# Attention over hop tokens in half-array products, and one iteration's statements in a written order

## The chip, the cores and the metric

One core of a Trainium2 chip runs the whole program. The metric is the device time of one execution in microseconds (us). The kernel before took 3996.6 us, the median of three runs from 3993.74 to 4000.15 us. The profile shows one execution, of 3999.62 us, with a span of 3997.8 us.

## The reference, cut to what matters

A graph of 10,000 nodes and 160,000 edges. Seven normalized propagations make seven more token rows for each node beside its input row, so each node has eight tokens of 128 numbers. One attention block runs over the eight tokens of each node by itself, and a second softmax weighs the eight results into one row.

```python
tok = jnp.stack(toks, axis=1)                      # (N, 8, 128)
t = _layernorm(tok)
q, key, v = t @ wq, t @ wk, t @ wv
attn = softmax(q @ key.T * scale)                  # 8 x 8 in each node
o = tok + (attn @ v) @ wo
r = _layernorm(o)
alpha = softmax(r @ w_r)                           # over the 8 tokens
return einsum('nk,nkd->nd', alpha, o)
```

## The kernel before, in words

The program has two stages. The class `Hops` makes the seven propagations, with the token rows written to `tok` in device memory; the change does not touch it. Behind it the function `attention` runs, and the change is all there, but for a few constants that are made during the hops.

`attention` works on groups of 16 nodes, which with eight tokens each fill 128 partitions (partition = 8 x node + token). Sixteen groups make a supergroup (`SG = 16`); there are 625 groups, so the list `sgs` has 40 supergroups, the first with one group and the others with sixteen. The loop at L1168 is a software pipeline over them. In iteration `i` it

- starts the loads of the token rows of supergroup `i+3` on the SyncE queue (`load`),
- transposes supergroup `i+1` on TensorE (`xT`, four parts of four groups) and ScalarE copies each part out of PSUM,
- for `i` makes the values (`val`, six parts of up to three groups, `xT` as the stationary operand and `Wv` as the moving one; columns 128 to 130 of `Wv` give three extra numbers for each token), the rows `uT` (four parts), the sums of squares (`squares`, sixteen ScalarE activations with an accumulator), and the scores (`score`, 32-column tiles of the array, four nodes to a tile),
- for `i-1` makes the softmax on VectorE (`soft1a`, `soft1b`, `soft2`, `soft2b`) with the exponential on ScalarE (`soft_exp`), spreads the weights by GpSimd over a product with `in4` (tile `p`, 32 wide), transposes the 32x32 blocks on VectorE, and has GpSimd copy the four diagonal blocks of each group into a 128x128 tile `PT` that is zero elsewhere (`soft3`, L1071),
- for `i-2` multiplies `PT` with the values (`attend`, sixteen 128x128x128 products) and adds the tokens on VectorE (`resid`, L989),
- for `i-3` takes the statistics of the result (`stats`, sixteen VectorE instructions), and the inverse roots for `i` and `i-3` together (`norms`, `root`, `norms2`),
- for `i-4` makes the second softmax (`read1`, `read_exp`, `read2`), and for `i-5` the weighted sum (`read3`, 32-column tiles) and the store.

The order of the work is that of the Python statements (`tc.manual_schedule`): each engine takes its instructions in the order in which they are written, and waits on semaphores where one needs another engine's result. `same_node` is a product that gives each row a sum over the eight rows of its node, in 32-column tiles (tile `sm`). PSUM has eight banks: three for `pt`, `pv` and `pu` together, two for `po`, and one each for `ps`, `sm` and `pf`.

Of the kernel before, what the change touches and what calls it, by code (L numbers as in the profile page):

```python
# [36 lines left out]
BIG = 32768.0  # L37

# [793 lines left out]
class Attention:  # L832
# [3 lines left out]
    def __init__(self, ctx, tc, tab, tok, ws, ngrp=N // 16):  # L836
        self.tc, self.nc, self.tok, self.ws = tc, tc.nc, tok, ws
        r = ngrp % SG
        self.sgs = [(0, r)] * (r > 0) + [(s, SG) for s in range(r, ngrp, SG)]

        y = [t.bitcast(F32)[:, a:a + SG, :] for t in tab[::-1] for a in range(0, NT - SG + 2, SG)]
        self.xb, self.ob = y[:6], y[6:]
        cp = ctx.enter_context(tc.tile_pool(name="acp", bufs=1))
        for name, w in (("M", 128), ("Wv", 131), ("id8", 8), ("in4", 4), ("sel", 16), ("same", 128), ("ident", 128)):
            setattr(self, name, cp.tile([128, w], F32, name=name))

# [3 lines left out]
    def load(self, i, ks=range(8), queue=None):  # L850
        s, n = self.sgs[i]
        for k in ks:
            src = bass.AP(tensor=self.tok[k].tensor, offset=self.tok[k].offset + s * 16 * 128, ap=[[n * 128, 16], [128, n], [1, 128]])
            (queue or self.nc.sync).dma_start(self.x(i)[k::8, :n, :], src)

    def constants(self, ctx, pw, ident):
# [3 lines left out]
        M, Wv, id8, in4, sel, same = self.M, self.Wv, self.id8, self.in4, self.sel, self.same  # L860
# [11 lines left out]
        pn, pk, pq = (cp.tile([128, 1], I32, name=n) for n in ("pn", "pk", "pq"))  # L872
# [3 lines left out]
        nf, kf, qf = (cp.tile([128, 1], F32, name=n) for n in ("nf", "kf", "qf"))  # L876
        for f, i in ((nf, pn), (kf, pk), (qf, pq)):
            V.tensor_copy(f, i)
# [5 lines left out]
        V.tensor_scalar(in4, cf[:, :4], qf, None, op0=ALU.is_equal)  # L884
        V.tensor_scalar(sel, cf, nf, None, op0=ALU.is_equal)
# [23 lines left out]
def attention(ctx, att, out):  # L909
# [7 lines left out]
    M, Wv, id8, in4, sel, same, ident = att.M, att.Wv, att.id8, att.in4, att.sel, att.same, att.ident  # L917
# [8 lines left out]
    PT, AB = [], []  # L926
    for i in range(2):
        p = cp.tile([128, SG, 128], F32, name=f"pT{i}")
        G.memset(p, 0.0)
        PT.append(p)  # L930
        a = cp.tile([128, SG, 32], F32, name=f"Ab{i}")
        G.memset(a, 0.0)
        AB.append(a)
# [30 lines left out]
    def val(i, c):  # L964
        a, b = 3 * c, min(3 * c + 3, sgs[i][1])
        if c == 0:
            S[i]["v"] = vp.tile([128, SG, 131], F32, name="v")
        if a >= b:
            return
        p = pp.tile([128, 512], F32, name="pv", tag="a", bufs=3)[:, :393].rearrange("p (g d) -> p g d", d=131)  # L970
        for g in range(a, b):
            T.matmul(p[:, g - a, :], S[i]["xT"][:, g, :], Wv, start=True, stop=True)  # L972
        A.copy(S[i]["v"][:, a:b, :], p[:, :b - a])

    def attend(i, q):
        a, b = 4 * q, min(4 * q + 4, sgs[i][1])
        if q == 0:
            S[i]["o"] = att.ob[i % len(att.ob)]
        if a >= b:
            return  # L980
        p = pp.tile([128, 4, 128], F32, name="po", tag="o", bufs=2)
        for g in range(a, b):
            T.matmul(p[:, g - a, :], PT[i % 2][:, g, :], S[i]["v"][:, g, :128], start=True, stop=True)  # L983
        S[i]["po", q] = p

    def resid(i, q):
        a, b = 4 * q, min(4 * q + 4, sgs[i][1])
        if a < b:
            V.tensor_tensor(S[i]["o"][:, a:b, :], S[i]["po", q][:, :b - a], S[i]["x"][:, a:b, :], op=ALU.add)  # L989

    def squares(i, a, b):

        if a == 0:
            S[i]["sq"] = sp.tile([128, SG], F32, name="sq")
        for g in range(a, min(b, sgs[i][1])):
            j = jp.tile([128, 128], F32, name="junk")
            A.activation(j, S[i]["x"][:, g, :], AF.Square, bias=S[i]["x"][:, g, 0:1], scale=-1.0, accum_out=S[i]["sq"][:, g:g + 1])  # L997

    def score(i):
        p = S[i]["s"] = pp.tile([128, SG, 32], F32, name="ps", tag="s", bufs=1)  # L1000
        for g in range(sgs[i][1]):
            for c in range(0, 128, 32):
                T.matmul(p[c:c + 32, g, :], S[i]["uT", g // 8][:, g % 8, c:c + 32], S[i]["xT"][:, g, c:c + 32],
                         start=True, stop=True, tile_position=(0, c))
# [6 lines left out]
    def extras(i):  # L1011

        n = sgs[i][1]
        r = wp.tile([128, 2, SG, 8], F32, name="rb")
        V.tensor_tensor(r[:, 0, :n], S[i]["rs"][:, :, None].to_broadcast([128, n, 8]), id8[:, None, :].to_broadcast([128, n, 8]), op=ALU.mult)
        V.tensor_tensor(r[:, 1, :n], S[i]["v"][:, :n, 128:129].to_broadcast([128, n, 8]), id8[:, None, :].to_broadcast([128, n, 8]), op=ALU.mult)
        S[i]["rb"] = r


    def soft1a(i):  # L1020
        n = sgs[i][1]
        c = wp.tile([128, SG, 4, 8], F32, name="c4")[:, :n]
        V.tensor_tensor(c, S[i]["s"][:, :n].rearrange("p g (n k) -> p g n k", k=8),
                        in4[:, None, :, None].to_broadcast([128, n, 4, 8]), op=ALU.mult)
        d = wp.tile([128, SG, 2, 8], F32, name="c2")[:, :n]
        V.tensor_tensor(d, c[:, :, 0:2], c[:, :, 2:4], op=ALU.add)
        e = S[i]["e"] = wp.tile([128, SG, 8], F32, name="e")[:, :n]
        V.tensor_tensor(e, d[:, :, 0], d[:, :, 1], op=ALU.add)

    def soft1b(i):  # L1030
        n = sgs[i][1]
        e = S[i]["e"]
        rk = wp.tile([128, SG, 8], F32, name="rk")[:, :n]
        V.tensor_tensor(rk, S[i]["sm"][:, 0, :n], S[i]["rs"][:, :, None].to_broadcast([128, n, 8]), op=ALU.mult)
        V.tensor_mul(e, e, rk)
        m = wp.tile([128, SG], F32, name="m")[:, :n]
        V.tensor_reduce(m, e, axis=X, op=ALU.max)
        V.tensor_tensor(e, e, m[:, :, None].to_broadcast([128, n, 8]), op=ALU.subtract)

    def soft_exp(i):  # L1040
        n = sgs[i][1]
        y = S[i]["y"] = wp.tile([128, SG, 9], F32, name="y")[:, :n]
        A.copy(y[:, :, 8:9], S[i]["v"][:, :n, 129:130])
        A.activation(S[i]["e"], S[i]["e"], AF.Exp)

    def soft2(i):
# [3 lines left out]
        V.tensor_reduce(z, e, axis=X, op=ALU.add)  # L1050
        V.reciprocal(z, z)
        V.tensor_tensor(e, e, S[i]["sm"][:, 0, :n], op=ALU.mult)
        V.tensor_tensor(e, e, z[:, :, None].to_broadcast([128, n, 8]), op=ALU.mult)  # L1053
        p = wp.tile([128, SG, 4, 8], F32, name="p4")[:, :n]
        G.tensor_tensor(p, e[:, :, None, :].to_broadcast([128, n, 4, 8]), in4[:, None, :, None].to_broadcast([128, n, 4, 8]), op=ALU.mult)  # L1055
        S[i]["p"] = p

    def soft2b(i):
# [3 lines left out]
        V.tensor_tensor(y[:, :, :8], S[i]["e"], S[i]["sm"][:, 1, :n], op=ALU.mult)  # L1062
        w = S[i]["w"] = sp.tile([128, SG], F32, name="w")[:, :n]
        V.tensor_reduce(w, y, axis=X, op=ALU.add)

    def soft3(i):
        n = sgs[i][1]
        t = wp.tile([128, SG * 32], F32, name="t4")
        V.transpose(t[:, :n * 32], S[i]["p"].rearrange("p g n k -> p (g n k)"))
        for c in range(0, 128, 32):  # L1070
            G.tensor_copy(PT[i % 2][c:c + 32, :n, c:c + 32], t[c:c + 32, :n * 32].rearrange("p (g k) -> p g k", k=32))  # L1071
# [8 lines left out]
    def norms(i, j):  # L1080
        v = sp.tile([128, 2, SG], F32, name="rv")
        if not (ok(i) and ok(j)) or min(sgs[i][1], sgs[j][1]) < SG:
            V.memset(v, 1.0)
        if ok(i):
            n = sgs[i][1]
            d = sp.tile([128, SG], F32, name="rx")[:, :n]
            V.tensor_mul(d, S[i]["v"][:, :n, 130], S[i]["v"][:, :n, 130])
            V.scalar_tensor_tensor(v[:, 0, :n], S[i]["sq"][:, :n], 1.0 / D, d, op0=ALU.mult, op1=ALU.subtract)
        if ok(j):
            n = sgs[j][1]  # L1090
            st = S[j]["st"][:, :n]
# [206 lines left out]
```

## Time and profile before

| | us |
|---|---|
| median of three runs | 3996.6 |
| the profiled execution, its span | 3999.62, 3997.8 |
| last matmul of the hops starts, first transposition of the attention | 3314.02, 3321.62 |
| score of the third supergroup, score of the last one | 3354.07, 3949.18 |
| busy over the span: PE, DVE, ACT, POOL | 3745.5, 3322.9, 2724.5, 1766.6 |

The attention takes some 680 us at the end of the span. PE is TensorE's matmul row, PEld its weight loads, DVE is VectorE, ACT ScalarE and POOL GpSimd. A row of the timeline gives a start, a busy time, the engine, the line, the operation with its tiles and shapes, and how many instructions are merged in it; the busy time of merged rows reaches beyond the start of the next row, because a matmul's end (and, to a smaller degree, a VectorE instruction's) overlaps with the next one's start. What a row costs its engine is therefore read from its start to the start of the next row.

### The profile page before, as it was taken

The numbers are of one execution on the slowest core, as the hardware profiler recorded it, in microseconds if no ns is written. First come the engines' busy times: TensorE is split into PE (matmuls) and PEld (weight loads), VectorE is DVE, ScalarE is ACT, GpSimd is POOL, SyncE is SP. The second block draws the span as 40 slices with busy tenths as digits, with TensorE's granted clock in tenths as the row PEclk, the third lists the DMA queues.
The fourth block names the chain that finished last, engine by engine and source line by source line (L and its number), as shares of the span: only waits on it lengthen the run. The fifth ranks groups of instructions, "written<-read, shape, count | busy, mean of one in ns | idle before, by whom it ended". The sixth has DMA issues, their size and how long they took to land.

```text
span 3997.8 us, 165094 instructions
## 1 busy us (share of the span) xinstructions
PE 3745.5 (94%) x69690; PEld 3031.4 (76%) x69690; DVE 3322.9 (83%) x6961; ACT 2724.5 (68%) x6830; POOL 1766.6 (44%) x2342
## 2 busy tenths in 40 slices
PE   6886799999989999999999999999999999999997
PEld 4665566666658888888888788878878887788885
DVE  8998999999977777777777777777766666999998
ACT  6884456666666666666666666666665658888884
POOL 0000333333335665666666566656656662222222
PEclk8998899999999999999999999999999999999998
DMA  3100445454556666666666666666656552222220
GB/s 104 32 2 1 134 151 154 149 162 143 156 168 189 201 201 193 202 203 200 193 202 202 185 202 202 202 189 198 202 184 205 186 183 77 74 74 76 78 78 13
DMA packets 321189, 594.93 MB, mean 149 GB/s; under 512 B 56183, under 2 KB 214101, under 8 KB 315189
## 3 DMA queue, kind: packets, MB, share of 16 engines
q1 hardware_dynamic: 282485, 506.62, 40.0%
q0 software_dynamic: 35392, 72.55, 6.3%
q8 instruction: 546, 8.95, 0.9%
q10 hardware_dynamic: 2560, 5.12, 0.4%
q14 instruction: 206, 1.69, 0.1%
HBM read 455.43 MB, written 128.67 MB: 146 GB/s over the span
## 4 chain that ended last, share of the span: by engine, by line
PE 71%; DVE 19%; ACT 4%; issue 2%; DMA 2%; POOL 0%; another core or an unknown queue 0%; SPq 0%; DVEq 0%; ACTq 0%; POOLq 0%
PE p L580 26%; PE acc L556 24%; PE acc L542 4%; DVE w L514 3%; PE pv L972 3%; PE po L983 3%; PE pu L961 3%; DVE ux L219 2%; DVE o L212 2%; ACT rs L340 2%; PE tb L440 2%; PE pt L951 1%; DVE oh L206 1%; DVE R L212 1%; DVE w L511 1%
## 5 line engine op out<-in xcount | busy, mean ns | idle before, releaser
L585 ACT CAST eb<-p 128x512 f16<-128x512 f32 x3065 | 1623.7, 596 | 645.4 <-PE p L580 404.3
L587 DVE TENSOR_TENSOR eb<-p,one 128x512 f16<-128x512 f32 x1912 | 1230.6, 685 | 332.2 <-PE acc L556 195.9
L580 PE MATMUL p<-tab,w 128*32 128x256 f16 x39816 | 1288.7, 274 | 44.2 <-issue 21.4
L556 PE MATMUL acc<-eb,w 128*128 128x256 f16 (+1 forms) x9954 | 1246.9, 274 | 8.4 <-DVE indeg L649 3.1
L580 PEld LDWEIGHTS <-w 128*32 128x32 fp8e4 x39816 | 1002.3, 96 | 261.3 <-issue 225.8
L556 PEld LDWEIGHTS <-w 128*128 128x128 fp8e4 x9954 | 954.3, 98 | 170.3 <-issue 54.9
L526 POOL DMA_INDIRECT og<-tabh,oidx x553 | 613.3, 1109 | 767.7 <-DVE vi L478 389.6
L526 POOL DMA_INDIRECT og<-tabd,oidx x541 | 586.3, 1084 | 640.2 <-PE acc L556 294.3
L625 POOL TENSOR_SCALAR r<-s,ctok 128x128 f32<-128x128 f32 x474 | 294.3, 621 | 47.7 <-DVE s L571 30.3
L616 ACT ACTIVATE tab<-s,c 128x128 f16<-128x128 f32 x395 | 158.6, 402 | 209.7 <-DVE eb L587 185.6
L617 DVE SCALAR_TENSOR_TENSOR tab<-s,c,tab 128x128 f16<-128x128 f32 x395 | 138.9, 352 | 180.8 <-issue 168.0
L571 DVE TENSOR_REDUCE s<-acc 128x128 f32<-128x256 f32 x553 | 228.7, 414 | 24.0 <-PE acc L569 11.2
L997 ACT ACTIVATE junk<-tab 128x128 f32<-128x128 f32 x625 | 245.1, 394 | 0.0
L340 ACT ACTIVATE rs<-iof,rb 128x128 fp8e4<-128x128 f32 x784 | 231.8, 389 | 0.3
L514 DVE TENSOR_TENSOR w<-dsl,iof 128x2432 fp8e4<-128x2432 f16 x79 | 211.5, 2678 | 0.0
L983 PEld LDWEIGHTS po<-v,pT 128*128 128x128 f32 x1250 | 159.5, 194 | 42.1 <-issue 27.7
L525 POOL COPY og<-eb 128x1 f16<-128x1 f16 x452 | 83.9, 186 | 241.7 <-ACT eb L585 241.7
L1055 POOL TENSOR_TENSOR p<-e,in 128x512 f32<-128x512 f32 (+1 forms) x40 | 40.8, 1020 | 321.0 <-DVE e L1053 321.0
L972 PE MATMUL pv<-Wv,xT 128*128 128x131 f32 x1250 | 176.7, 285 | 1.3 <-ACT xT L952 0.6
L983 PE MATMUL po<-v,pT 128*128 128x128 f32 x1250 | 167.0, 277 | 5.5 <-DVE tab L989 4.1
L972 PEld LDWEIGHTS pv<-Wv,xT 128*128 128x128 f32 x1250 | 154.2, 192 | 17.9 <-issue 8.8
L542 PE MATMUL acc<-og,w 128*128 128x256 f16 x553 | 156.8, 284 | 0.0
(285 smaller groups left out, 4611.9 us busy)
## 6 DMA issues: line engine op xcount, KB each, us to landing
w<-gsd SPq DMA_DIRECT2D x474, 592.0 KB
gsd<-w SPq DMA_DIRECT2D x79, 592.0 KB
rb<-srow SPq DMA_DIRECT2D x79, 576.0 KB
tok<-r SPq DMA_DIRECT2D x546, 64.0 KB
tab<-tok SPq DMA_DIRECT2D x273, 128.0 KB
tabd<-tab SPq DMA_DIRECT2D x396, 64.0 KB
og<-tabh,oidx POOLq DMA_INDIRECT x553
og<-tabd,oidx POOLq DMA_INDIRECT x541
```

Source lines behind the costliest of these rows:

```text
L340: A.activation(ro[:, j - a, i, :], self.iof, AF.Abs_reciprocal_sqrt, scale=2.0 ** 21, bias=rb[:, j - VP, i:i + 1], saturate=False)
L514: V.tensor_tensor(w[:, :NJ * 128].rearrange("p (j d) -> p j d", d=128), dsl[:, g, :, None].to_broadcast([128, NJ, 128]), self.iof1[:, None ...
L526: self.nc.gpsimd.indirect_dma_start(out=o, out_offset=None, in_=src[0] if i == NI else src[1], in_offset=bass.IndirectOffsetOnAxis(ap=self ...
L542: T.matmul(acc[0][:, :256], W, og[i], start=start, stop=stop)
L556: T.matmul(acc[0][:, :m], w[:, J * 128:(J + 1) * 128], e[:, j, :m], start=first and J == 0, stop=J == NG - 1 and not (first or late))
L580: T.matmul(p[32 * q:32 * q + 32, j], w[:, NJ * 128 + s * CAP:NJ * 128 + (s + 1) * CAP], tab[:, s, :], start=True, stop=True)
L585: A.copy(e[:, :n, 0:256], pv)
L587: V.tensor_tensor(e[:, :n, 0:256], pv, self.one[:, :, None].to_broadcast([128, n, 256]), op=ALU.mult)
L625: self.nc.gpsimd.tensor_scalar(r, s, ct[:, t:t + 1], None, op0=ALU.mult)
L972: T.matmul(p[:, g - a, :], S[i]["xT"][:, g, :], Wv, start=True, stop=True)
L983: T.matmul(p[:, g - a, :], PT[i % 2][:, g, :], S[i]["v"][:, g, :128], start=True, stop=True)
L997: A.activation(j, S[i]["x"][:, g, :], AF.Square, bias=S[i]["x"][:, g, 0:1], scale=-1.0, accum_out=S[i]["sq"][:, g:g + 1])
```

## The change

Four things.

1. **Products of eight nodes.** A full supergroup's sixteen groups are split into two halves of eight groups. A unit `u = c * 8 + q` holds, on partitions 0 to 63, nodes `8c` to `8c+7` of group `q`, and on partitions 64 to 127 the same nodes of group `8 + q`. `val` writes values in this layout with two 64-column products for each unit, `score` reads its tiles in it, the weights are spread eight wide with `in8` (tile `p8`, 64 numbers for each unit, in place of 32), and VectorE transposes them. The transposed tile `t8` is used directly: a 64x64 block of it is zero off the node's own 8x8 blocks. `attend` makes four 64x64 products, each with 128 moving columns, for each `q`. `PT`, its zeroing and the GpSimd copies are gone.
2. **Regrouping.** Sums of squares are taken by group and the softmax sums by unit, so both go to a tile `R`, and four 64-column products with parts of the identity (`regroup`) bring the one into unit order and the other into group order, in a part of the bank of `pf`.
3. **A written order.** The functions return short steps, and `ORDER` names the order in which one iteration issues them; the loop reads it word by word. `score` and the first step of the softmax now belong to the start of the next iteration, `xT` to its middle.
4. **Smaller things.** The copy of one column of `v` into `y` goes from ScalarE to GpSimd. The first supergroup has two groups, of which one is stored.

```diff
+ORDER = """
+v0 b b s b a0 b q q v1 v2 q v3 b q v4 v5 b b m h b b a1 q b q a2 a3 r0 a4 a5
+a6 e r1 t0 r2 b c0 o00 k q c2 c1 x0 o01 x1 q q c3 f w0 q d0 b d1 b b b q u0 u1 b t1
+o10 w1 n0 q n3 n1 n2 g w2 n4 n5 p n6 x2 x3 u2 u3 o11 q q q y0 y1 z0 z1 z2 z5 z3 q z6 z4
+"""
...
-        self.sgs = [(0, r)] * (r > 0) + [(s, SG) for s in range(r, ngrp, SG)]
+        self.sgs = [(0, 2)] * (r > 0) + [(s, SG) for s in range(r, ngrp, SG)]
...
-    PT, AB = [], []
+    R = []
+    for i in range(6):
+        a = cp.tile([128, 2, SG], F32, name=f"R{i}")
...
     def val(i, b):
-        for g in range(a, b):
-            T.matmul(p[:, g - a, :], S[i]["xT"][:, g, :], Wv, start=True, stop=True)
+        for u in us:
+            c, q = u // m, u % m
+            for h in range(2):
+                T.matmul(p[64 * h:64 * h + 64, u - us[0], :], S[i]["xT"][:, h * m + q, 64 * c:64 * c + 64], Wv,
+                         start=True, stop=True, tile_position=(0, 64 * h))
...
-        p = pp.tile([128, 4, 128], F32, name="po", tag="o", bufs=2)
-        for g in range(a, b):
-            T.matmul(p[:, g - a, :], PT[i % 2][:, g, :], S[i]["v"][:, g, :128], start=True, stop=True)
+        for h in range(2):
+            S[i]["po", s, h] = pp.tile([128, 4, 128], F32, name="po", tag="o", bufs=2)
+        for q in qs:
+            for c in range(2):
+                for h in range(2):
+                    a, z, u = 64 * h, 64 * c, c * m + q
+                    T.matmul(S[i]["po", s, h][z:z + 64, q - 4 * s, :], t[a:a + 64, u * 64:u * 64 + 64], v[a:a + 64, u, :128],
+                             start=True, stop=True, tile_position=(a, z))
...
+    def regroup(out, rr, moves):
+        for m, js in moves:
+            js = slice(js[0], js[-1] + 1)
+            for b in range(2):
+                for a in range(2):
+                    T.matmul(out[64 * a:64 * a + 64, js, b * m:b * m + m], ident[:, 64 * b:64 * b + 64], rr[:, js, a * m:a * m + m],
+                             start=True, stop=True, tile_position=(0, 64 * a))
...
     def soft_exp(i):
-        A.copy(y[:, :, 8:9], S[i]["v"][:, :n, 129:130])
+        G.tensor_copy(y[:, :, 8:9], S[i]["v"][:, :n, 129:130])
...
-        G.tensor_tensor(p, e[:, :, None, :].to_broadcast([128, n, 4, 8]), in4[:, None, :, None].to_broadcast([128, n, 4, 8]), op=ALU.mult)
+            G.tensor_tensor(p, e[:, :, None, :].to_broadcast([128, n, 8, 8]), in8[:, None, :, None].to_broadcast([128, n, 8, 8]), op=ALU.mult)
...
     def soft3(i):
-        t = wp.tile([128, SG * 32], F32, name="t4")
-        V.transpose(t[:, :n * 32], S[i]["p"].rearrange("p g n k -> p (g n k)"))
-        for c in range(0, 128, 32):
-            G.tensor_copy(PT[i % 2][c:c + 32, :n, c:c + 32], t[c:c + 32, :n * 32].rearrange("p (g k) -> p g k", k=32))
+        t = S[i]["t"] = wp.tile([128, SG * 64], F32, name="t8")
+        V.transpose(t[:, :n * 64], S[i]["p"].rearrange("p g n k -> p (g n k)"))
...
+        single = dict(s=(soft, score, i - 1), e=(soft, soft_exp, i - 1), p=(soft, soft3, i - 1), f=(read, read_exp, i - 4),
+                      g=(ok(i - 5), store, i - 5))
+        several = dict(v=(ok(i), val, i), u=(ok(i), uT, i), t=(ok(i - 2), attend, i - 2))
+        lists = dict(a=(soft, soft1, i - 1), c=(soft, soft2, i - 1), d=(soft, soft2b, i - 1), r=(read, read1, i - 4),
+                     w=(read, read2, i - 4), n=(True, norms, i, i - 3), y=(True, root, i), z=(True, rstd, i, i - 3))
+        plain = dict(q=square, b=stat, m=sums, h=weigh, k=move)
```

The words of `ORDER`: `v`, `u`, `x`, `t` are the parts of `val`, `uT`, `xT` and `attend`; `s`, `m`, `h`, `k` are `score`, the node sums, the weighted sum of `read3` and the regrouping; `b` is one of the sixteen statistics and `q` one of the sixteen squares (six of this supergroup ahead of `k`, ten of the next behind it); `o` is `resid`; `a`, `c`, `d` are steps of the first softmax, with `e` its exponential and `p` the transposition; `r`, `f`, `w` are those of the second; `n`, `y`, `z` make the inverse roots; `g` is the store.

More of the change, by code (lines that the diff above doesn't have):

```diff
@@ L1167, in attention @@
     load(1)
+    S += [dict() for _ in range(5)]
+    taken = [0, 0]
     for i in range(-1, n + 5):
@@ L1171, in attention, with square, stat @@
             load(i + 3)
-        if ok(i - 1):
-            soft1a(i - 1)
-        for q in range(4):
+        soft, read = ok(i - 1), ok(i - 4)
+        taken = [taken[1] if i >= 0 else 0, 0]
+        done, current, kept = [0], [0], {}
+        def square():
+            j = current[0]
+            if ok(i + j):
+                squares(i + j, taken[j], taken[j] + 1)
+            taken[j] += 1
+        def stat():
+            if ok(i - 3):
+                stats(i - 3, done[0], done[0] + 1)
+            done[0] += 1
```

337 lines of the change are left out of this document (168 added, 169 removed).

## The prediction

> **What bounds the kernel now.** I read the page's first two parts, then the busy times of a long stretch of the attention, the waits in it, the chain that ended last, and one iteration in order of time. The page says that PE is the busiest engine and that the last fifth of the span, the attention, is another regime than the hops:
>
> ```profile
> PE 3745.5 (94%) x69690; PEld 3031.4 (76%) x69690; DVE 3322.9 (83%) x6961; ACT 2724.5 (68%) x6830; POOL 1766.6 (44%) x2342
> ...
> PE   6886799999989999999999999999999999999997
> DVE  8998999999977777777777777777766666999998
> ACT  6884456666666666666666666666665658888884
> ```
>
> In its steady part (windows, then waits of the same stretch, then the chain's lines behind 3400) the engines stand like this:
>
> ```profile
> 3400.00:3900.00 500.00, 493.06 (x8180) 402.78 (x8179) 474.91 (x1670) 442.34 (x1641) 130.74 (x215) 1.00 0.26 76
> ...
> PE pt L951 <- PE ps L1003: 6.5, 31, 0.3
> ...
> DVE tab L989 <- PE po L983: 0.7, 2, 0.5
> ...
> by line: PE pv L972 18.6%; PE po L983 17.0%; PE pu L961 16.0%; PE pt L951 9.1%; PE ps L1003 5.8%; PE pf L1151 5.6%; DVE st L1078 4.3%; PE sm L1009 4.0%; DVE tab L989 3.2%; issue 1.9%; DMA tab<-in_x 1.3%; DVE rv L1097 0.8%; DVE t L1069 0.7%;
> ```
>
> PE is busy 493 of 500 us, and its one wait is 0.2 us an iteration. The chain is three quarters PE. But VectorE is busy 475 of 500 and waits 0.7 us on PE in all of it: its missing 25 us are seams between its own instructions. So both are full, and ScalarE (442) is close. A gain on PE counts only if VectorE shrinks with it. The period comes from the scores of the third and the last supergroup, 37 iterations apart: (3949.18 - 3354.07) / 37 = 16.08 us.
>
> ```profile
> 3354.07 1.62 PE L1003 MATMUL ps<-xT,uT 128*32 128x32 f32 x128
> ...
> 3949.18 1.30 PE L1003 MATMUL ps<-xT,uT 128*32 128x32 f32 x128
> ```
>
> **PE, term by term.** Most of one iteration's matmuls, to be read from start to start:
>
> ```profile
> 3606.70 1.05 PE L983 MATMUL po<-v,pT 128*128 128x128 f32 x8
> 3607.59 0.60 PE L951 MATMUL pt<-ident,tab 128*128 128x128 f32 x4
> 3608.03 1.88 PE L961 MATMUL pu<-xT,M 128*128 128x512 f32 x4
> 3609.75 1.05 PE L983 MATMUL po<-v,pT 128*128 128x128 f32 x8
> 3610.73 1.30 PE L1003 MATMUL ps<-xT,uT 128*32 128x32 f32 x128
> 3612.24 0.63 PE L951 MATMUL pt<-ident,tab 128*128 128x128 f32 x4 [0.22 <-PE ps L1003]
> 3612.71 0.83 PE L972 MATMUL pv<-Wv,xT 128*128 128x131 f32 x6
> 3613.47 0.64 PE L1009 MATMUL sm<-rb,same 128*32 128x256 f32 x8
> 3613.93 0.40 PE L1009 MATMUL sm<-lb,same 128*32 128x128 f32 x8
> 3614.26 0.94 PE L972 MATMUL pv<-Wv,xT 128*128 128x131 f32 x6
> 3615.13 1.08 PE L1151 MATMUL pf<-tab,Ab 128*32 128x128 f32 x32
> 3616.14 0.94 PE L972 MATMUL pv<-Wv,xT 128*128 128x131 f32 x6
> 3616.91 1.05 PE L983 MATMUL po<-v,pT 128*128 128x128 f32 x8
> ```
>
> *Attend.* Eight matmuls take 3607.59 - 3606.70 = 0.89 us, 0.111 each; an iteration has 32 (sixteen products, two passes each), 3.56 us. After, there are 64 quarter-size ones (eight `q`, four tiles, two passes) with the same 128 columns. Four tiles of 32 columns do run side by side here: the 32 of `pf` take 1.01 us, 0.13 for each round of four. If the four 64x64 tiles do so too, attend is 16 rounds of 0.111, 1.78 us: a gain of 1.78. No row here shows tiles that share columns and differ in rows, so the bounds are 1.78 gained and nothing gained (only the column halves overlap); a serial array would lose 3.56. I take the first, nearest to the `pf` row.
>
> The Trainium skill (TensorEngine Tiling (Array Packing), Key Properties) says that different tiles can load weights and multiply in parallel, and counts four independent ones at 64x64, which would give the 1.78. No run here shows it yet.
>
> *Val.* Twice as many matmuls, of 64 columns, two at a time over 131 moving columns: 32 rounds as before, no change. Score, sums, `read3`, `xT` and `uT` keep their counts.
>
> *Changes of tile shape.* They cost here: the eight `po` ahead of the scores take 0.98 instead of 0.89, the six `pv` ahead of the sums 0.76, and behind `read3` 0.77, instead of 0.67 (6 x 0.111); the 32 of `pf` take 0.14 more than eight rounds of 0.109. That is 0.09 to 0.10 into, and 0.14 plus 0.10 out of, a small shape: about 0.33 a pair, 0.165 each. Before, six in an iteration; after (v0, s, v1, m, t0, k, x0, t1, x2) nine: +0.5. Against it, the first transposition's wait behind the scores (0.22, for the loads' semaphores) now comes behind `k` and can go. Net +0.3, bounds 0 and +0.6.
>
> *Regroup.* Two products on each column half, two passes each, make four rounds of 16 columns. The scores' 32 rounds of 32 columns take 1.51, 0.05 each, so 0.2, to 0.4 if each costs a `pf` round; I take 0.25. It also makes PE wait for the last two squares before it, with x0 to u3 queued behind it. Ahead of it stand the sums (0.79), `read3` (1.01) and half of attend (0.9), 2.7 us behind v5, while ScalarE has a copy and two squares to do, 1.3 by the rows below. No cost.
>
> PE's sum: 16.08 - 1.78 + 0.3 + 0.25 = **14.85 us** a period.
>
> **VectorE.** The rows of one iteration, and then one of the last iterations, where no GpSimd copies run:
>
> ```profile
> 3600.39 1.64 DVE L1078 BATCH_NORM_STATS2 st<-tab 128x6 f32<-128x128 f32 x8
> ...
> 3607.73 2.55 POOL L1071 COPY pT<-t 32x512 f32<-32x512 f32 x4 [3.04 <-DVE rx L1087]
> 3607.77 0.60 DVE L1088 SCALAR_TENSOR_TENSOR rv<-sq,rx 128x16 f32<-128x16 f32 x1
> 3608.50 0.51 DVE L1094 SCALAR_TENSOR_TENSOR rd<-rd 128x16 f32<-128x16 f32 x1
> 3609.14 0.51 DVE L1096 SCALAR_TENSOR_TENSOR rv<-rv,rd 128x16 f32<-128x16 f32 x1
> 3609.68 0.64 DVE L1097 TENSOR_SCALAR rv<-rv 128x32 f32<-128x32 f32 x1
> 3610.23 0.27 DVE L1136 TENSOR_REDUCE rz<-re 128x16 f32<-128x128 f32 x1
> 3610.53 0.25 DVE L1137 RECIPROCAL rz<-rz 128x16 f32<-128x16 f32 x1
> ...
> 3976.33 0.18 DVE L1096 SCALAR_TENSOR_TENSOR rv<-rv,rd 128x16 f32<-128x16 f32 x1
> 3976.54 0.18 DVE L1097 TENSOR_SCALAR rv<-rv 128x32 f32<-128x32 f32 x1
> ```
>
> Under the four GpSimd copies four short instructions take 2.26 us; without them 0.18 each, 0.72. The copies go: -1.5. The products for `Ab` (0.77 us of GpSimd, issued at w2) will still lie over n4 and n5, as now over two others: 0.
>
> A step that needs its predecessor starts after it has ended (0.30 behind a 0.27 reduce), while independent ones start 0.08 before the end (eight statistics in 1.64): 0.11 a seam. Some 19 of VectorE's 55 instructions are such followers now. In the written order I count five whose input is the step right before (a5, a6, z1, z2, z5), since statistics and other chains stand between the rest: -14 x 0.11 = -1.5.
>
> The transposition doubles:
>
> ```profile
> L1069 DVE STREAM_TRANSPOSE t<-p x40: 211/701/711, 3335.1 to 3963.2; 128x512 f32<-128x512 f32 x39, 128x32 f32<-128x32 f32 x1
> ...
> L1055 POOL TENSOR_TENSOR p<-e,in x40: 241/1040/1042, 3334.8 to 3960.0; 128x512 f32<-128x512 f32 x39, 128x32 f32<-128x32 f32 x1
> ```
>
> From 32 to 512 elements it grows by 0.49, so 512 more cost +0.5. VectorE: 16.08 - 1.5 - 1.5 + 0.5 = 13.6, seams included.
>
> **ScalarE and GpSimd.** The window of one iteration and ScalarE's rows in it:
>
> ```profile
> 3600.39:3616.58 16.19, 15.97 (x267) 13.04 (x266) 15.43 (x55) 14.31 (x53) 4.24 (x7) 1.00 0.28 75
> ...
> 3599.86 0.21 ACT L1043 COPY y<-v 128x16 f32<-128x16 f32 x1
> 3601.54 0.40 ACT L997 ACTIVATE junk<-tab 128x128 f32<-128x128 f32 x1
> 3601.84 0.19 ACT L997 ACTIVATION_READ_ACCUMULATOR junk<-tab 128x1 f32 x1
> 3602.96 0.49 ACT L973 COPY v<-pv 128x393 f32<-128x393 f32 x1
> ```
>
> ScalarE loses the `y` copy: 14.31 - 0.21 = 14.1. GpSimd goes from 4.24 to 4.24 - 2.55 + 0.8 (`p8` twice as wide: 1.04 - 0.24 from 32 to 512, so 1.84) + 0.2 = 2.7. The store's two transfers are queued on SyncE behind the loads still, only later in the iteration; nothing waits for them before the end.
>
> **The sum.** PE remains the longest, 14.85 against 14.1 and 13.6. At the points where one engine waits for another, the order leaves slack: a3 needs the sums, which PE gives at 6.4 us of its iteration (v0 0.7, scores 1.5, v1 to v5 3.4, sums 0.8). VectorE's work behind t1 (o10 to z4) is some 5.5 us and t1 ends near 12.2, so VectorE is 2.8 us into the next iteration when it begins there, and its 3.5 us of steps ahead of a3 bring it to about the same time; its spare 1.2 us takes up what is missing. 37 periods x (16.08 - 14.85) = 45.5. The lead-in of two short iterations gains nothing. Of the five iterations behind the last scores two have the stretched instructions, -3.0, and give 1.5 back on the transposition and shape changes: -1.5. 3999.6 - 47 = 3952.6 for the profiled execution, which stood 3.0 above the median: **3950**.
>
> **Rivals.**
>
> *PE keeps its full time (slower).* If the two row halves of the array take turns, the gain of 1.78 is gone, and 0.3 + 0.25 stay: 16.63 a period, +20, so 4017. It decides from the point where attend's 64 matmuls take over 3.0 us instead of 1.78. For it: no such tiles in this trace. Against: the halves write to two `po` banks, so they share no output. 0.07; with all four in turn it would be 4150.
>
> *VectorE or ScalarE becomes the bound.* Place: z0 needs y1, and ScalarE has four copies and three squares queued ahead of y0; or `p8` holds VectorE. Price: one late chain of 0.7 us an iteration, 15.55 a period, 3976. For it: only 0.75 us stand between PE and ScalarE. Against: the squares can be done while PE runs sums, `read3` and attend. 0.2. One version has a rule beside it: if GpSimd's 1.84 us product held one VectorE instruction to its end, as the 0.6 us copies do, VectorE would have 13.6 + 1.8 = 15.4, so 3970.
> The Trainium skill (SBUF — State Buffer, in its terms on the shared port pair) has it as an exclusive lock, held for the whole instruction. The stretched rows agree (0.51 against 0.18).
>
> *More than the sum.* Shape changes at 0.1 and the wait gone: 16.08 - 1.78 + 0.1 + 0.2 - 0.2 = 14.4, and ScalarE fits under it: 3934. 0.13.
>
> *The change does little:* waits eat all but 0.2 us: 3990 to 4004. 0.05.
>
> **How the numbers follow.** The sum's own case has 0.55 and reaches from 3938 to 3966 (PE between 14.5 and 15.2). The range goes on to the faster case and the late-chain case, 3925 to 3985, leaving out the two cases of no gain and the ends. Measurements of this kernel differ by some 0.2% (8 us). Faster by more: 0.55 + 0.2 + 0.13 = 0.88; within: 0.05; slower: 0.07.
>
> **What would show it.** Right: period near 14.9; attend in two rows of 32 matmuls, each near 0.9 us; the four short VectorE instructions at 0.2 to 0.4; PE still without waits; ScalarE at 94% of a period. Wrong: attend near 1.8 us a half; VectorE waits of over 0.3 us at the first step behind the sums or at z0; PE waits at `k` on squares, or on copies out of the three shared banks.

## The result, and the profile after

The changed kernel takes 3966.7 us, the median of four runs from 3961.11 to 3971.59, against 3997.2 us for the kernel before beside it (3993.74 to 4000.15): a ratio of 0.9925, with a 95% interval from 0.9909 to 0.9941, so 30.5 us less. The profiled execution is the shortest of the four, 3961.11 us. Other chips gave the kernel before other times (3938.8, 3942.8 and 3997.7 us in the sessions below), so every experiment is given as a ratio to the kernel before on its own chip.

The page of the kernel after, its span and first part, shows TensorE with 2871 more matmuls in less busy time, VectorE with 89 us less, and little change on ScalarE:

```profile
span 3959.3 us, 170861 instructions
...
PE 3702.7 (94%) x72561; PEld 2949.4 (74%) x72561; DVE 3233.9 (82%) x6966; ACT 2703.9 (68%) x6792; POOL 1712.6 (43%) x2221
```

The busy times of the same steady stretch as before, then lines from its list of waits (engine, line, what was waited for: sum, times, longest):

```profile
3400.00:3900.00 500.00, 494.71 (x10925) 361.93 (x10922) 422.53 (x1765) 445.24 (x1697) 94.18 (x129) 1.00 0.26 76
...
DVE rz L1161 <- ACT ry L1136: 46.2, 32, 1.5
...
PEld pu L978 <- ACT xT L969: 34.4, 65, 0.9
...
ACT e L1073 <- DVE e L1067: 33.5, 32, 1.2
```

TensorE is as busy as before, 495 of 500 us, but now its weight loads wait for ScalarE's copies of `xT`, ScalarE waits for VectorE, and VectorE waits for ScalarE, a ring through three engines. The length of the period can be read from the scores of the third and the last supergroup:

```profile
3354.22 0.36 PE L1043 MATMUL ps<-xT,uT 128*32 128x32 f32 x20
...
3916.33 0.36 PE L1043 MATMUL ps<-xT,uT 128*32 128x32 f32 x20
```

They stand (3916.33 - 3354.22) / 37 = 15.19 us apart, against 16.08: 33.0 us over the 37 periods. Behind the last scores 43.0 us are left, against 48.6: another 5.6 us. The third scores start 0.15 us later than before, so that makes the 38.5 us by which the two profiled spans differ (3997.8 to 3959.3).

One iteration of TensorE in order of time, to be read from start to start (its period is a long one, 15.34 us, because of 0.28 us lost among the values ahead of the first row; the rows shown are as in the others):

```profile
3601.39 0.64 PE L1049 MATMUL sm<-rb,same 128*32 128x256 f32 x8
3601.85 0.40 PE L1049 MATMUL sm<-lb,same 128*32 128x128 f32 x8
3602.07 1.06 PE L1202 MATMUL pf<-tab,Ab 128*32 128x128 f32 x32
3603.05 1.10 PE L1013 MATMUL po<-v,t 64*64 64x128 f32 x32
3604.09 0.41 PE L1028 MATMUL pf<-R,ident 128*64 128x16 f32 x8
3604.43 1.09 PE L968 MATMUL pt<-ident,tab 128*128 128x128 f32 x8
3605.36 1.88 PE L978 MATMUL pu<-xT,M 128*128 128x512 f32 x4
3607.17 1.11 PE L1013 MATMUL po<-v,t 64*64 64x128 f32 x32
3608.21 1.09 PE L968 MATMUL pt<-ident,tab 128*128 128x128 f32 x8
3609.14 2.14 PE L978 MATMUL pu<-xT,M 128*128 128x512 f32 x4
3611.21 0.89 PE L994 MATMUL pv<-Wv,xT 128*64 128x131 f32 x12
3612.03 1.46 PE L1043 MATMUL ps<-xT,uT 128*32 128x32 f32 x128
```

Each half of `attend` takes 1.04 us (3603.05 to 3604.09), and two pairs of `pu` that do the same work take 1.81 (3605.36 to 3607.17) and 2.07 us (3609.14 to 3611.21). The second pair is held up for 0.26 us. What ScalarE does meanwhile:

```profile
3605.12 1.08 ACT L969 COPY xT<-pt 128x512 f32<-128x512 f32 x2 [0.29 <-PE pt L968]
...
3607.85 1.06 ACT L979 COPY uT<-pu 128x512 f32<-128x512 f32 x2
...
3609.19 0.43 ACT L1213 COPY f<-pf 128x128 f32<-128x128 f32 x2
3609.49 1.10 ACT L969 COPY xT<-pt 128x512 f32<-128x512 f32 x2
```

Between its copies of x1 and x2 ScalarE has five squares, an exponential, two copies of `uT` and the two of `f` to do. x2 is in its bank by about 3608.7, but the copy starts at 3609.49; u3 is the fourth user of the three shared banks behind x2, x3 and u2, so it waits for that copy.

Most periods are 15.06 us long. But among 24 periods from the middle of the attention nine are longer by 0.25 to 1.15 us, and their mean is 15.31; before, only one of 24 stood out, and their mean was 16.19. In a long one TensorE stands still among the values or the scores, mostly with no releaser:

```profile
3841.32 1.44 PE L1043 MATMUL ps<-xT,uT 128*32 128x32 f32 x128
3842.68 0.44 PE L994 MATMUL pv<-Wv,xT 128*64 128x131 f32 x2
3843.72 2.45 PE L994 MATMUL pv<-Wv,xT 128*64 128x131 f32 x40 [0.60 <-issue]
```

"issue" means that the engine waited for nothing that the profile shows.

### The profile page after: what moved, and what is told of

Read it like the earlier page. It is cut to its first block, busy times and chain, and to the rows that moved or that the text cites. A ratio compares the mean times of both kernels' runs of the same rounds, so it can differ in the third digit from the quotient of the medians.

```text
span 3959.3 us, 170861 instructions
## 1 busy us (share of the span) xinstructions
PE 3702.7 (94%) x72561; PEld 2949.4 (74%) x72561; DVE 3233.9 (82%) x6966; ACT 2703.9 (68%) x6792; POOL 1712.6 (43%) x2221
## 4 chain that ended last, share of the span: by engine, by line
PE 72%; DVE 18%; ACT 4%; DMA 3%; issue 2%; SPq 0%; ACTq 0%; DVEq 0%; POOLq 0%
PE p L587 26%; PE acc L563 24%; PE acc L549 4%; PE pu L978 3%; PE pv L994 3%; DVE w L521 3%; DVE ux L226 2%; PE po L1013 2%; PE pt L968 2%; DVE o L219 2%; DVE oh L213 2%; ACT rs L347 2%; DVE R L219 1%; PE tb L447 1%; DVE w L518 1%
## 5 line engine op out<-in xcount | busy, mean ns | idle before, releaser
L1083 POOL TENSOR_TENSOR p<-e,in 128x1024 f32<-128x1024 f32 (+1 forms) x40 | 76.5, 1913 | 445.9 <-DVE e L1082 420.2
L994 PEld LDWEIGHTS pv<-Wv,xT 128*64 128x64 f32 x2504 | 138.6, 137 | 44.1 <-ACT uT L979 29.1
L994 PE MATMUL pv<-Wv,xT 128*64 128x131 f32 x2504 | 163.2, 280 | 8.0 <-issue 3.3
L978 PE MATMUL pu<-xT,M 128*128 128x512 f32 (+1 forms) x314 | 157.1, 606 | 0.1
L230 PEld LDWEIGHTS <-id 128*128 128x128 f16 x1040 | 101.9, 102 | 58.8 <-issue 31.6
```

What stands on the lines that cost most here:

```text
L978: T.matmul(p[:, :b - a], M, S[i]["xT"][:, a:b, :], start=True, stop=True)
L994: T.matmul(p[64 * h:64 * h + 64, u - us[0], :], S[i]["xT"][:, h * m + q, 64 * c:64 * c + 64], Wv, start=True, stop=True, tile_position=(0, ...
```

## The experiments

The theory after the result: the new products save TensorE what was said, the written order is needed to let them, and two things take some of it back, ScalarE's queue between the copies (0.26 us a period) and the pauses (0.25 a period). Rivals: the order alone made the gain; or the 15.06 us are TensorE's own work and no wait; or the ring through VectorE sets the period. The numbers below are of 24 periods from the middle of each kernel's attention; "longer" counts those more than 0.2 us above the median.

| kernel | ratio to before, 95% interval | median period | mean | longer | matmuls per iteration |
|---|---|---|---|---|---|
| before | 1 | 16.17 | 16.19 | 1 | 264 |
| after | 0.9925 [0.9909, 0.9941] | 15.06 | 15.31 | 9 | 336 |
| after, second session | 0.9932 [0.9920, 0.9944] | 15.08 | 15.38 | 9 | 336 |
| order alone | 0.9977 [0.9967, 0.9986] | 15.89 | 15.92 | 1 | 264 |
| products alone, first transcription | 1.0368 [1.0353, 1.0382] | 20.11 | 19.81 | 2 | 336 |
| products alone, second | 1.0111 [1.0095, 1.0126] | 17.22 | 17.24 | 0 | 336 |
| one spare square | 0.9971 [0.9960, 0.9983] | 15.45 | 15.73 | 9 | 336 |
| three squares moved | 0.9932 [0.9917, 0.9946] | 15.14 | 15.31 | 7 | 336 |
| two squares moved | 0.9908 [0.9894, 0.9922] | 14.86 | 15.18 | 10 | 336 |
| scores late | 1.0136 [1.0120, 1.0153] | 17.62 | 17.58 | 10 | 336 |
| scores late, two squares moved | 1.0110 [1.0096, 1.0125] | 17.36 | 17.26 | 9 | 336 |
| whole-width values | 0.9903 [0.9886, 0.9920] | 15.10 | 15.13 | 2 | 304 |
| whole-width values, two squares moved | 0.9888 [0.9873, 0.9903] | 14.84 | 14.85 | 0 | 304 |

**The order alone.** The kernel after with the old products put back: `PT`, the 32-wide spread and the GpSimd copies, values by group and no regrouping; the written order stays.

```diff
-                    T.matmul(S[i]["po", s, h][z:z + 64, q - 4 * s, :], t[a:a + 64, u * 64:u * 64 + 64], v[a:a + 64, u, :128],
-                             start=True, stop=True, tile_position=(a, z))
+                T.matmul(p[:, g - a, :], PT[i % 2][:, g, :], S[i]["v"][:, g, :128], start=True, stop=True)
...
+            G.tensor_copy(PT[i % 2][c:c + 32, :n, c:c + 32], t[c:c + 32, :n * 32].rearrange("p (g k) -> p g k", k=32))
```

> The 128x128 products of before (with the zeroed tile PT and GpSimd's diagonal copies, the 32-wide spread and transposition, groups instead of units, no regrouping) in the written order of after. TensorE keeps attend at 3.56 us a period, so by its own sum (16.13 of before, less 0.15 for the wait behind the scores and 0.1 for one tile shape less behind the sums) it stays near 15.9: 37 x 0.2 = 7 us less in the steady part, and the end may be some 4 us shorter, since the written order has fewer followers on VectorE: 3985 to 3992. Rival, that the order is the larger part of the gain: 3975 or less. Pauses of TensorE of over 0.56 us that wait for nothing: 0 to 2 in 500 us if they come from the number of matmuls (267 an iteration again), 9 or 10 as in after if they come from the order (the scores among the values).

The ratio is 0.9977 and the period 15.89. Its window:

```profile
3400.00:3800.00 400.00, 399.27 (x6618) 332.50 (x6618) 313.46 (x1360) 344.94 (x1310) 111.22 (x201) 1.00 0.27 77
```

The 15.89 is what was expected. TensorE is busy 399 of 400 us, its matmuls wait only once in that window (0.7 us), and the other engines have room (VectorE 78% busy, 95% in the kernel before), so TensorE's own work sets the pace there. In the groups of the same window two of the instructions that were stretched to 0.51 and 0.64 us before have means of 169 and 235 ns:

```profile
L1121 DVE TENSOR_SCALAR rv<-rv 128x32 f32<-128x32 f32 x25 | 5.9, 235 | 0.0
...
L1115 DVE SCALAR_TENSOR_TENSOR rv<-rv,rd 128x16 f32<-128x16 f32 x25 | 4.2, 169 | 0.0
```

The order by itself takes away 0.28 us of 16.17 a period; the other 0.83 us of the median need the products. It also shortens the end: 43.9 us are left behind the last scores, against 48.6 before and 43.0 with the products.

**The products alone.** The kernel after with `ORDER` rewritten as the old order of statements; the two halves of `attend` and the regrouping, which the old order doesn't have, were put where they fit.

```diff
-v0 b b s b a0 b q q v1 v2 q v3 b q v4 v5 b b m h b b a1 q b q a2 a3 r0 a4 a5
...
+s a0 a1 a2 x0 v0 q q m a3 a4 a5 a6 v1 q e q h v2 q q t0 b b b b b b b b o00 c0 c2 c1 c3 d0 d1 r0 r1 r2
+x1 v3 g v4 v5 f q k b b b b b b b b o01 p x2 u0 q q u1 q t1 n1 n4 n0 n2 n3 n5 n6 w0 w1 w2
+x3 u2 q u3 y0 y1 q q q q q z0 z1 z2 z3 z4 z5 z6 o10 o11
```

> The new products and the regrouping, in the order of before (stated in the words of ORDER; attend in two halves, at the first and the third quarter). If the products alone free TensorE, the period is bound next by VectorE, which has lost the stretched instructions (-1.5) and has the longer transposition (+0.5) but keeps its 19 followers: near 15.1 to 15.3, so 3960 to 3968, like after. Rival, that the short steps are needed: one engine's long blocks hold another, the period stays at 15.7 or more, 3983 or later.

It is 3.7% slower than before, which none of the numbers held. From its waits behind 3500:

```profile
DVE rz L1161 <- ACT ry L1136: 85.6, 21, 4.5
...
PE pf L1028 <- ACT junk L1035: 40.4, 20, 2.0
```

TensorE waits 2.0 us at the regrouping for the last square, and VectorE 4.1 at z0. That is a fault of my place for `k`, so it went behind u0 in a second transcription, with the last square ahead of the copy of `f`:

```diff
-x1 v3 g v4 v5 f q k b b b b b b b b o01 p x2 u0 q q u1 q t1 n1 n4 n0 n2 n3 n5 n6 w0 w1 w2
+x1 v3 g v4 v5 q f b b b b b b b b o01 p x2 u0 k q q u1 q t1 n1 n4 n0 n2 n3 n5 n6 w0 w1 w2
```

> The new products in the order of before once more, with the sixteenth square ahead of f and the regrouping behind u0. In products_only TensorE waited 2.0 us an iteration at the regrouping for the last square, which stood behind f, and VectorE 4.1 us for y1. If that misplaced wait was all of its 20.1 us, the period falls to 15.1 to 15.6, ratio 0.99 to 1.0; if the long blocks of the old order do not carry the new products, it stays above 16.1 and the ratio above 1.0.

Still 1.1% slower than before, at 17.2 us. From its order of time on TensorE:

```profile
3609.63 0.43 PE L1013 MATMUL po<-v,t 64*64 64x128 f32 x2
3610.49 1.10 PE L1013 MATMUL po<-v,t 64*64 64x128 f32 x30 [0.43 <-DVE tab L1020]
...
3613.83 0.53 PE L1043 MATMUL ps<-xT,uT 128*32 128x32 f32 x36
3614.58 1.00 PE L1043 MATMUL ps<-xT,uT 128*32 128x32 f32 x92 [0.22 <-ACT uT L979]
```

The second half of `attend` waits for VectorE to empty its bank (by medians it takes 1.89 us, against 1.04 for the first), and the scores for the last copy of `uT`, which comes right before them in this order (1.92 us against 1.36 in the kernel after). So the products without the order lose, in the two places for `k` that were tried; how much of the 17.2 is the old order and how much my transcription stays open.

**One spare square.** A square more on ScalarE, whose result nobody uses, behind the two behind x1:

```diff
-a6 e r1 t0 r2 b c0 o00 k q c2 c1 x0 o01 x1 q q c3 f w0 q d0 b d1 b b b q u0 u1 b t1
+a6 e r1 t0 r2 b c0 o00 k q c2 c1 x0 o01 x1 q q j c3 f w0 q d0 b d1 b b b q u0 u1 b t1
```

> Kernel after with one spare square an iteration (its sum goes to an unused tile) behind the two that stand behind x1. Theories 1 and 3: the period grows by about one square, 0.39 us, so 37 x 0.39 = 14 us later than after, 3978 to 3984. Theory 2: ScalarE has 1.4 us to spare, no change, 3962 to 3970.

The median period grows from 15.06 to 15.45, about the square's own time (the ScalarE rows of the kernel after go from one square to the next in 0.38 us). Its rows:

```profile
3602.87 1.30 PE L968 MATMUL pt<-ident,tab 128*128 128x128 f32 x8
3604.01 2.31 PE L978 MATMUL pu<-xT,M 128*128 128x512 f32 x4
3606.25 0.89 PE L994 MATMUL pv<-Wv,xT 128*64 128x131 f32 x12
```

x2 and x3 take 1.14 us instead of 0.93, and u2 and u3 2.24 instead of 2.07. What ScalarE gets to do at this place comes back whole as waits of TensorE, which it would not if the 15.06 us were TensorE's own work.

**Three squares moved.** In the kernel after ScalarE waits 1.05 us an iteration at `e` (33.5 us in 32 times). Three squares go there from between the copies:

```diff
-a6 e r1 t0 r2 b c0 o00 k q c2 c1 x0 o01 x1 q q c3 f w0 q d0 b d1 b b b q u0 u1 b t1
+a6 q q q e r1 t0 r2 b c0 o00 k q c2 c1 x0 o01 x1 c3 f w0 d0 b d1 b b b q u0 u1 b t1
```

> Kernel after with three of the sixteen squares moved from between ScalarE's copies (two behind x1, one behind f) to right ahead of e, where ScalarE waits 1.1 us for VectorE. Theory 1, ScalarE's work between the first and the last copies of xT (five squares, f, uT, the store) keeps the shared PSUM banks and holds TensorE at u2 and u3: pu's second row goes from 2.07 to below 1.8 us, the regular period from 15.06 to 14.6 to 14.75, the time 12 to 17 us below after: 3950 to 3955. Theory 2, TensorE's own matmuls set 15.06 and ScalarE is merely in step: no change, 3962 to 3970. Theory 3, the loop from y1 through VectorE to e and back through ScalarE: shorter by the three squares too, as in theory 1, until TensorE's 14.6 ends it.

No change against the kernel after: 0.9932. The rows:

```profile
3606.06 0.44 PE L1028 MATMUL pf<-R,ident 128*64 128x16 f32 x8
3606.54 1.06 PE L968 MATMUL pt<-ident,tab 128*128 128x128 f32 x8
...
3611.22 1.88 PE L978 MATMUL pu<-xT,M 128*128 128x512 f32 x4
3613.03 0.89 PE L994 MATMUL pv<-Wv,xT 128*64 128x131 f32 x12
```

u2 and u3 are back at 1.81 us, but the regrouping takes 0.48 us in these rows and 0.58 in the median (0.34 in the kernel after): the third moved square is the sixteenth of its supergroup, which `k` needs, and it is now late. The wait has changed place. My figure for TensorE's own work was also too low: without the wait it is 15.06 - 0.26 = 14.80.

**Two squares moved.** The same with two.

```diff
-a6 e r1 t0 r2 b c0 o00 k q c2 c1 x0 o01 x1 q q c3 f w0 q d0 b d1 b b b q u0 u1 b t1
+a6 q q e r1 t0 r2 b c0 o00 k q c2 c1 x0 o01 x1 c3 f w0 q d0 b d1 b b b q u0 u1 b t1
```

> Two squares moved ahead of e, not three. With three, TensorE's wait at u2 and u3 (0.26 us) went and one of 0.25 came at k, for the sixteenth square; with none, k has some 0.9 us to spare. If ScalarE's place for the squares is all that holds TensorE above the sum of its own rows (14.81 without the wait), two leave both waits at nothing: regular period 14.81 to 14.87, some 8 us below after_again. If it is the loop through VectorE (y1, z, a, e) that sets 15.06 to 15.13, the period stays there.

The median period is 14.86, and the time 3904.24 us against 3914.92 of the kernel after on the same chip, 10.7 less (the intervals of the two ratios just overlap, so the periods carry this more than the times).

```profile
3612.24 0.41 PE L1028 MATMUL pf<-R,ident 128*64 128x16 f32 x8
3612.58 1.09 PE L968 MATMUL pt<-ident,tab 128*128 128x128 f32 x8
3613.51 1.88 PE L978 MATMUL pu<-xT,M 128*128 128x512 f32 x4
3615.32 1.10 PE L1013 MATMUL po<-v,t 64*64 64x128 f32 x32
```

The regrouping takes 0.34 and the pair of `pu` 1.81. With the spare square this shows ScalarE's queue between the copies as the cause of the 0.26 us, from both sides. The pauses stay: ten of 24 periods are long.

These runs don't part that queue from the ring through VectorE, which holds the same squares; the rows of the kernel after do. In the iteration shown above, with 0.28 us lost by TensorE, ScalarE's exponential starts 7.31 us behind the scores, as in the regular ones (7.30). But the copy of x0 behind it starts at 8.43 us and not at 8.15, after 0.29 us of waiting for TensorE, and the whole period is 0.28 us longer. So TensorE's x0, and not VectorE, releases ScalarE there.

The kernel after ran again beside the two squares:

> The changed kernel as it is, beside the next ones on one chip: ratio to the kernel before 0.991 to 0.994, regular period 15.06.

It repeated its ratio, 0.9932, its median period of 15.08 and its nine long periods.

**The scores late.** The pauses lie in the scores or among the values behind them. Here the scores stand behind all values, which also puts VectorE's first steps later:

```diff
-v0 b b s b a0 b q q v1 v2 q v3 b q v4 v5 b b m h b b a1 q b q a2 a3 r0 a4 a5
-a6 e r1 t0 r2 b c0 o00 k q c2 c1 x0 o01 x1 q q c3 f w0 q d0 b d1 b b b q u0 u1 b t1
+v0 b b b q q v1 v2 b q v3 b b q v4 v5 s b b m h b a0 q b q a1 r0 a2 a3 r1 a4 r2 a5
+a6 e t0 b o00 c0 k q c2 c1 x0 o01 x1 q q c3 f w0 q d0 b d1 b b b q u0 u1 b t1
```

> The scores moved from between v0 and v1 to right ahead of the sums, so that the three 32-column parts (scores, sums, read3) follow each other: two changes of tile shape less, 0.25 to 0.33 us of TensorE by the prediction's 0.165 each. VectorE's statistics stand ahead of a0, so that the later scores cost it little. If TensorE's own time counts, the regular period is 14.75 to 14.85; if ScalarE's section holds it, TensorE waits 0.25 longer at u2 and the period stays at 15.06. Pauses: as many as in after if they come from the number of TensorE's instructions, fewer if from the scores being among the values.

> Both moves together: 14.81 less 0.25 to 0.33, so 14.5 to 14.6, if TensorE's own time is what is left; ratio to before near 0.985 with the pauses of after. If a loop through VectorE or ScalarE takes over, 14.75 or more.

Both miss: 1.4% and 1.1% slower than before. From the first one's order of time:

```profile
3606.62 0.89 PE L994 MATMUL pv<-Wv,xT 128*64 128x131 f32 x12 [0.81 <-ACT v L996]
3607.77 1.11 PE L994 MATMUL pv<-Wv,xT 128*64 128x131 f32 x16 [0.26 <-ACT v L996]
...
3610.68 0.62 PE L1202 MATMUL pf<-tab,Ab 128*32 128x128 f32 x12
3613.55 0.85 PE L1202 MATMUL pf<-tab,Ab 128*32 128x128 f32 x20 [2.25 <-issue]
```

The values now wait for ScalarE's copies of values: the scores write to a bank of their own, and behind v0 they gave ScalarE 1.4 us to empty the shared ones. That wait is 29.9 us in 500, about 1.05 a period. The pauses moved along with the scores, to the sums, `read3` and `attend` behind them (seven at `read3` in 500 us), and one lasts 2.25 us. They also grew, to 23.3 us in 500, about 0.8 a period against 0.25; the rest of the 2.3 us that the mean period gained was not taken apart. The two squares are worth 0.3 us a period here as well.

**Values at whole width.** ScalarE's copy of `xT` writes the unit order, so that each unit's values come from one product of 128 columns: 32 matmuls an iteration fewer, and no change of tile shape ahead of v0. The scores read their tiles in that order too (not shown); nothing else differs from the kernel after.

```diff
-        A.copy(S[i]["xT"][:, a:b, :], p[:, :b - a])
+            A.copy(S[i]["xT"][:, :2 * m, 64 * h:64 * h + 64].rearrange("p (c q) d -> p c q d", c=2)[:, :, c - h * m:d - h * m, :],
+                   p[:, c - a:d - a, :].rearrange("p g (c d) -> p c g d", c=2))
...
-                T.matmul(p[64 * h:64 * h + 64, u - us[0], :], S[i]["xT"][:, h * m + q, 64 * c:64 * c + 64], Wv,
-                         start=True, stop=True, tile_position=(0, 64 * h))
+            T.matmul(p[:, u - us[0], :], S[i]["xT"][:, u, :], Wv, start=True, stop=True)
```

> ScalarE's copy of xT out of PSUM writes the units next to each other, so that val has one 128-column product for each unit again: 304 matmuls an iteration instead of 336, and no change of tile shape between u3 and v0. The rest as in after. The regular period is held by ScalarE at 15.06 and stays there, 15.0 to 15.06 (longer if the strided copy costs ScalarE time). If the pauses of TensorE come from the number of its instructions (each begins some 1.6 us behind the start of a 16 KB packet of the instruction queue), there are fewer than the 9 to 16 in 500 us of after, and the median falls by some 5 us or more; if not, as many and no change.

The median period stays, at 15.10, but the mean falls from 15.31 to 15.13: two of 24 periods are long, by 0.37 and 0.35 us, instead of nine. Over 37 periods that is 6.4 us, and the ratio is 0.9903 against 0.9925; the intervals of the two overlap, so the gain itself rests on the periods more than on the times.

With both, this and the two squares:

> The same with two squares moved ahead of e as in squares_two. TensorE's own sum is 14.81 less the change of tile shape (0.15): regular period 14.65 to 14.75. With fewer pauses the ratio to before is 0.986 to 0.988, with as many 0.989.

0.9888, 3950.82 us beside 3997.66: the shortest ratio of all. Its window and three rows:

```profile
3400.00:3900.00 500.00, 499.93 (x10285) 388.54 (x10284) 434.27 (x1818) 465.33 (x1754) 95.98 (x135) 1.00 0.27 77
...
3609.33 0.83 PE L997 MATMUL pv<-Wv,xT 128*128 128x131 f32 x6
3610.09 1.44 PE L1044 MATMUL ps<-xT,uT 128*32 128x32 f32 x128
3611.46 3.31 PE L997 MATMUL pv<-Wv,xT 128*128 128x131 f32 x26
3614.70 0.64 PE L1050 MATMUL sm<-rb,same 128*32 128x256 f32 x8
```

No period is long, and TensorE is busy 499.93 of 500 us. The period is 14.84 and not the lower one expected: the values take 0.76 + 3.24 = 4.00 us here, against 3.89 with the halves (medians of 0.82 and 3.07), so what the missing change of shape ahead of v0 saves is spent on the values themselves.

## Why the prediction was right, and where it was not

The direction and the mechanism held. The measured median is 16.7 us above the forecast and inside its range. By its own steps:

*TensorE's sum: right.* Without the 0.26 us wait a regular period is 14.80 us, where 14.85 was said, and moving two squares gave 14.86. (The 14.85 starts from 16.08, a mean that holds the short periods at the ends; the regular period before was 16.17.) The terms are nearly right as well. By medians of start to start over the steady part, `attend` went from 3.66 us to 2 x 1.035 = 2.07, its shape changes included, and the regrouping takes 0.34. Other parts come to -0.09: the scores lose 0.14, as the 0.22 us wait behind them is gone, the sums 0.11, the values 0.09 and `read3` 0.02, while `xT` gains 0.08 and `uT`, without its wait, 0.19. That makes -1.34, where -1.78 + 0.3 + 0.25 = -1.23 stood.

*The rival that the row halves take turns: refuted.* The 32 matmuls of a half of `attend` take 1.04 us. Eight rounds of four at 0.111 are 0.89, and the rest is the shape change; two at a time would be 1.78. So the rule of the Trainium skill (TensorEngine Tiling (Array Packing), Key Properties), that different tiles work in parallel, held here for tiles that differ in rows as well.

*VectorE: right, and a little better.* The short instructions that the GpSimd copies had stretched, and the transposition, in the kernel after:

```profile
3609.76 0.17 DVE L1120 SCALAR_TENSOR_TENSOR rd<-rd 128x16 f32<-128x16 f32 x1
...
3610.12 1.24 DVE L1101 STREAM_TRANSPOSE t<-p 128x1024 f32<-128x1024 f32 x1
3611.28 0.14 DVE L1128 TENSOR_SCALAR rv<-rv 128x32 f32<-128x32 f32 x1
```

The short ones take 0.14 to 0.17 us, against 0.51 to 0.64, and the transposition 1.24 (0.71 + 0.5 was said). VectorE's waits in the 500 us sum to 68.0, so its own work with seams is (500 - 68.0) / 33 = 13.1 us an iteration, against 13.6. The wait at z0 is there (46.2 us in 32 times, 1.44 each), as the late-chain rival had it; VectorE has the spare time for it. One reason was only half right: that the stretch ends because the GpSimd copies go. With the order alone they are still there (2.55 us an iteration), and the short instructions are short already, because they are done before the copies start: under these VectorE adds tokens and then waits for ScalarE.

*"At the points where one engine waits for another, the order leaves slack": wrong at one place.* That paragraph looked at a3 and at z0, and the regrouping's squares, but not at u3. ScalarE's own work is smaller than said, (500 - 52.3 of waits) / 33 = 13.6 us against 14.1, but 3.4 us of it stand in a row between the copies of x1 and x2 that empty the shared banks. The list of what would show it wrong had "copies out of the three shared banks", and that is what came: 0.26 us a period, where the rival's price was 0.7.

*Nothing in the sum stood for the pauses.* They cost 15.31 - 15.06 = 0.25 us a period in the middle, where the kernel before lost 0.02. "PE still without waits" held for the waits that a profile names, and not for these.

The account of the steady part: 16.17 - 14.80 = 1.37, less 0.26, less 0.25 - 0.02, is 0.88 us; times 37 that is 32.6, and 33.0 was measured where 45.5 was forecast. *The tail* gave 5.6 where 1.5 was said. The shortened periods at the two ends are in neither term. The order gave most of the tail, 48.6 to 43.9 us without the products; what in the order did it was not tried. So the forecast of the profiled execution is only 8.5 us too low, 12.5 in the steady part less some 4 in the tail, and that these two offset each other is luck. The other three runs are 3 to 10 us longer than the profiled one; the trace of one execution can't show where, so that part of the miss stays open.

What is shown of the pauses: moving the scores moves them and makes them more, and taking 32 of 336 matmuls away removes most of them without a change of the regular period. The traces also tell what TensorE waits for. In 400 us of the kernel after, the larger of its two instruction queues moved (packets, MB, share of the 16 DMA engines):

```profile
q8 instruction: 69, 1.13, 1.2%
```

These are 69 packets of 16 KB, against 63 in the kernel with whole-width values and 52 in the kernel before: in each, one packet to some 255 of the matmuls and weight loads that TensorE issued. In the kernel after eight matmuls between 3340 and 3960 us start behind a pause of over 0.25 us without a releaser. From each to the next TensorE takes 2048, 2048, 5376, 2048, 4096, 3328 and 2048 instructions (matmuls, weight loads and four semaphore instructions an iteration), each time a multiple of 256, and each starts 2.4 to 2.9 us after the start of such a packet. With the scores late it is the same, with 24 pauses and 23 multiples. So TensorE has come to the end of what it holds and waits for its next 256 instructions. The 336 matmuls and as many weight loads of an iteration are 2.6 packets, and 2048 instructions are three iterations, which is why about every third is long. The scores alone are 256 instructions in 1.36 us, less than those 2.4 us. What delays a packet is open, as no run changed the loading itself, and the number of matmuls does not decide alone: the second transcription has 336 as well, in 17.2 us, and no long period.

## What to carry to other kernels

When several producers share PSUM banks, list for the engine that empties them everything that stands in its queue between two copies: the bank, not the engine's total, sets the time, and one spare or two moved instructions at that place show it within a run. Work that writes to a bank of its own, such as the scores here, is also time for another engine; moving it can cost more than the stall it was moved for. Many short matmuls in a row have a price beyond their own time, since their instructions must be loaded too: where TensorE pauses without a releaser, count instructions from pause to pause. A busy share near 100% does not say that an engine is the bound (495 of 500 us here with 0.5 us a period lost): read its rows from start to start, against the same work elsewhere in the iteration.

## What the runs showed of the hardware

- Four 64x64 products of fp32 with 128 moving columns run at once: 32 matmuls in 1.04 us, eight rounds of 0.111 us and 0.15 us for the change of shape.
- With 336 matmuls in 15 us TensorE paused without a releaser in about every third iteration, which made that one 0.25 to 1.15 us longer; with 304 in 14.84 us it did not in the 24 periods read. The pauses stand a multiple of 256 instructions apart (7 of 7 distances in the kernel after), and each ends 2.4 to 2.9 us after a 16 KB packet of instructions starts.
- A product of 128 columns for both halves of the values is not cheaper than two of 64 columns side by side: 4.00 us against 3.89 an iteration.
